# When the main heads' decay is laid out: after the seventh early step, not after the third

## The chip, the cores and the metric

The kernel runs on one core of one Trainium2 chip. The metric is device time in microseconds (us) of one launch. A core has five engines that work side by side and wait for each other through semaphores: TensorE (PE, matrix products), VectorE (DVE), ScalarE (ACT), GpSimd (POOL) and SyncE (SP), whose queue here issues every transfer (DMA).

## The reference

Attention with a forgetting gate on 8 batches of 8 heads, 576 positions and width 64, and behind it a feed-forward network on all 4608 tokens:

```python
scores = scale * np.matmul(q, k.transpose(0, 1, 3, 2))
log_f = np.log(np.clip(f, 0.0001, 1.0))
cum = np.cumsum(log_f, axis=-1)
decay = cum[:, :, :, None] - cum[:, :, None, :]
scores = np.where(causal, -1000000000.0, scores + decay)
...                                   # softmax over keys
attn_out = np.matmul(attn, v)
h = x @ w_in                          # x: 4608 x 512, w_in: 512 x 2048
g = np.maximum(0.01 * h, h)
return g @ w_out                      # w_out: 2048 x 512
```

The decay depends on `f` alone. Its running sum `cum` of a head is all that the scores need of it.

## The kernel before, in words

**Two phases.** The feed-forward network is most of TensorE's work, and it needs attention's results first. So the kernel begins with *early steps*: for the first 256 positions of three batches (`NE` = 3), one step for each pair of heads, twelve steps in all (`g` counts the four pairs of a batch). What these give is enough for the first feed-forward groups. Then come the *main heads*: 64 tasks, one a head, for the remaining positions, with feed-forward work filled in between.

**An early step.** `early_scores(b, g)` makes four score tiles (`sce_b_g_c`): a product of `qk` (L109, in float32) and one that adds the decay (L109, from the tile `both`). DVE takes each out of PSUM with its minimum (L303, into `ze`), which frees one of only two banks for the next score tile; ACT exponentiates (L307), DVE makes the reciprocal of the sums (L312, L313) and ACT scales the four tiles (L315). `early_values(b, g)` runs one step later: PE transposes the tiles (`tre`, L113), ACT copies them out of PSUM (`pte`, L327), PE multiplies by the values (`ave`, four matmuls that each copy `pte` feeds two of), ACT and DVE split the result into a high and a low part (`xh` L340, `xl` L341), from which the feed-forward network reads.

**Weights.** Between steps, `load_weight` unpacks one piece of the feed-forward weights (16 pieces of 1 MB, two transfers each, L163): two passes on ACT (L177 into `wt`, L185 into `win_h` or `wout_h`) and five on DVE (L180, L186, L187, L190, L191).

**Feed-forward quanta.** `fill(n)` sends up to `n` pieces of the feed-forward network: `h` matmuls (24 for a tile), then `g` (ACT L631), its split `gh` (DVE L634) and `gl` (DVE L636), then `o` matmuls. `FQ` is zero for the first four steps and then 4, 8, 8, ... `warm(n)` sends matmuls on zeros whose result nobody reads; they stand between the scores of the first six steps.

**The decay's second layout.** The early steps use the two tiles in `both`, made at the start. The main heads read the decay from DRAM instead, and `decay_rows` puts it there: it scales the running sums `fc` in place (DVE L226), takes each block's first value off (five DVE instructions, L231, into `start`), splits both into a high and a low part (ACT L209 and DVE L210 for `fck`, the same for `fcq`) and writes four halves to DRAM (SP L238, `dec_k` and `dec_q`). The first transfers that read them back belong to `split(0)` (L382, L383), called in the eleventh step; the first matmul on the tile that they fill starts at 151.5 us.

**What sets the order.** The code above gives a program order, and a scheduler in the language's framework reorders each engine's instructions by its own estimate of when operands and buffers are ready. A few instructions are pinned to program order; L226 is one. Each engine then runs its list strictly in that order, so an instruction that waits holds all that stand behind it.

```python
if x == 2:
    decay_rows()
if x:
    early_values(*steps[x - 1])
```

Of the kernel before, what the change touches and what calls it, by code (L numbers as in the profile page):

```python
# [38 lines left out]
def forgetting_attention_ffn(ctx, tc, qT, kT, v4, vr, f, w_in, w_out, out):  # L39
# [155 lines left out]
    def weights(n):  # L195
        while len(loaded) < min(n, len(wpieces)):
            load_weight(len(loaded))
# [25 lines left out]
    def decay_rows():  # L223

        tc.keep_in_program_order(
            nc.vector.tensor_scalar(fc, fc, -1.0 / SCALE, None, op0=ALU.mult)  # L226
        )
        start = one.tile([P, S], F32, tag="x", name="start")
        for i in range(NCH):
            c = slice(i * P, width(i))  # L230
            nc.vector.tensor_scalar(  # L231
                start[:, c], fc[:, c], 0.0, fc[:, i * P:i * P + 1], op0=ALU.mult, op1=ALU.subtract
            )
        for name, tag, x, to in (("fck", "s1", fc, dec_k), ("fcq", "m1", start, dec_q)):
            r = one.tile([P, S], F32R, tag=tag, name=name, bufs=2)
            halves(r, x)
            for w in range(2):
                nc.sync.dma_start(to[:, w], r[w * NHEAD:(w + 1) * NHEAD].bitcast(F32))  # L238
# [4 lines left out]
    def load(t):  # L243

        s, c0, c1 = tasks[t]
        h = state[t] = {}
        a, n = c0 * P, S
        x = h["raw"] = one.tile([P, S], F32, tag="qraw", name=f"raw_{t}")
        for y, src in ((x[:D, a:n], qT[s][:, a:n]), (x[D:, :n], kT[s][:, :n])):
            last = nc.sync.dma_start(y, src)  # L250
            if t < 2:
                tc.keep_in_program_order(last)
        if s % 2 == 0:
            pairs[s // 2, c0] = {}

    def load_v(t):

        g, o = tasks[t][0] // 2, tasks[t][0] % 2
        vm = fixed["vm"]
        for y, src in ((vm[:, :NFULL], v4[g][:, o]), (vm[:REST, NFULL], vr[g][:, o])):  # L260
            last = nc.sync.dma_start(y, src)
            if t < 1:
                tc.keep_in_program_order(last)
# [3 lines left out]
    def early_load(b, g):  # L267

        e = early[b, g] = {}
        x = e["qk"] = one.tile([P, 2, T], F32, tag="b2", name=f"qk_{b}_{g}", bufs=B2)  # L270
        for y, src in enumerate((qT, kT)):
            nc.sync.dma_start(
                x[:, y], src[b * HPB + 2 * g:b * HPB + 2 * g + 2, :, :T].rearrange("s d n -> (s d) n")
            )
        v = e["v"] = one.tile([P, 2, T // P, D], F32, tag="b2", name=f"ve_{b}_{g}", bufs=B2)
        nc.sync.dma_start(v, v4[b * HPB // 2 + g][:, :, :T // P])

    def early_scores(b, g):
        e = early[b, g]
        mx = one.tile([P, 4], F32, tag="max", name=f"maxe_{b}_{g}", bufs=3)  # L280
        sm = one.tile([P, 4], F32, tag="sum", name=f"sume_{b}_{g}", bufs=3)
        for i in range(2):
            n = width(i)
            ps = [
                psum.tile([P, 512], F32, tag="sc", name=f"sce_{b}_{g}_{2 * o + i}")[:, :n]
                for o in range(2)
            ]
            for o in range(2):
                x = e["qk"][o * D:(o + 1) * D]
                matmul(ps[o], x[:, 0, i * P:n], x[:, 1, :n], start=True, stop=False)  # L290
            for o in range(2):
                s = b * HPB + 2 * g + o
                matmul(
                    ps[o], pick[:, s:s + 1].broadcast_to([P, P]), decay_r[i],
                    start=False, stop=True,
                )
            for o in range(2):
                c = 2 * o + i
                tag = ZE[g % 2][c]
                z = e[c] = one.tile(  # L300
                    [P, n], F32, tag=tag, name=f"ze_{b}_{g}_{c}", bufs=BUFS.get(tag, 1)
                )
                nc.vector.tensor_tensor_reduce(  # L303
                    out=z, in0=ps[o], in1=tri[:, TRI - n:], scale=-SCALE, scalar=3.0e38,
                    op0=ALU.add, op1=ALU.min, accum_out=mx[:, c:c + 1],
                )
                nc.scalar.activation(  # L307
                    z, z, AF.Exp, bias=mx[:, c:c + 1], scale=-1.0, accum_out=sm[:, c:c + 1]
                )
            if b * HPB // 2 + g < WARM[2]:  # L310
                warm(WARM[1])
        nc.vector.tensor_scalar(sm, sm, 1.0e-9, None, op0=ALU.add)  # L312
        nc.vector.reciprocal(sm, sm)  # L313
        for c in range(4):
            nc.scalar.activation(e[c], e[c], AF.Copy, scale=sm[:, c:c + 1])  # L315

    def early_values(b, g):
        e = early[b, g]
        pts = []
        for o in range(2):  # L320
            ps = psum.tile([P, 512], F32, tag="tr", name=f"tre_{b}_{g}_{o}")
            for x, (c, j) in enumerate(((2 * o, 0), (2 * o + 1, 0), (2 * o + 1, 1))):
                transpose(
                    ps[:, x * P:(x + 1) * P], e[c][:, j * P:(j + 1) * P], ident
                )
            pt = one.tile([P, 3 * P], F32, tag=("z4", "e4")[o], name=f"pte_{b}_{g}_{o}")
            nc.scalar.copy(pt, ps[:, :3 * P])  # L327
            pts.append(pt)
        out = psum.tile([P, 512], F32, tag="tr", name=f"ave_{b}_{g}")
        for o, pt in enumerate(pts):  # L330
            rows_ = slice(o * D, (o + 1) * D)
            matmul(out[rows_, :T], e["v"][:, o, 0], pt[:, :T], start=True, stop=False)
            matmul(out[rows_, P:T], e["v"][:, o, 1], pt[:, T:], start=False, stop=True)
        if b not in groups:
            x = one.tile([P, T], F32, tag="x", name=f"xe_{b}_{g}")
            nc.scalar.copy(x, out[:, :T])
            nc.sync.dma_start(xd[g * P:(g + 1) * P, b * T:(b + 1) * T], x)
            return
        xh, xl = groups[b]
        nc.scalar.copy(xh[:, g, :], out[:, :T])  # L340
        nc.vector.tensor_tensor(xl[:, g, :], out[:, :T], xh[:, g, :].bitcast(F32), op=ALU.subtract)  # L341
# [22 lines left out]
    def split(t):  # L364


        s, c0, c1 = tasks[t]
        h = state[t]
        a, n = c0 * P, S
        x = "ab"[t % 2]  # L370
        s1 = h["s1"] = one.tile([P, S], F32R, tag="s1", name=f"s1_{t}", bufs=2)
        m1 = h["m1"] = one.tile([P, S], F32R, tag="m1", name=f"m1_{t}", bufs=2)
        s2, m2 = h["s2"], h["m2"] = fixed["s2" + x], fixed["m2" + x]
        raw = h["raw"]
        for y, x in ((s1[:D, a:n], raw[:D, a:n]), (m1[D:, :n], raw[D:, :n])):
            last = nc.scalar.copy(y, x)  # L376
            if t < 2:
                tc.keep_in_program_order(last)
        for y in (s1, s2):
            nc.sync.dma_start(y[D:, a:n].bitcast(F32), s1[:D, a:n].bitcast(F32))  # L380
        nc.sync.dma_start(m1[:D, :n].bitcast(F32), m1[D:, :n].bitcast(F32))
        nc.sync.dma_start(s2[2:4, a:n].bitcast(F32), dec_q[s][:, a:n])  # L382
        nc.sync.dma_start(m2[:2, :n].bitcast(F32), dec_k[s][:, :n])  # L383
        minus(m2[D:, :n], raw[D:, :n], m1[D:, :n].bitcast(F32))
        minus(s1[:D, a:n], raw[:D, a:n], s1[:D, a:n].bitcast(F32))
# [291 lines left out]
    def fill(n):  # L677

        settle()
        credit[0] += n  # L680
        while credit[0] >= 1:
            credit[0] -= 1
            if not next(quanta, None):
                credit[0] = 0
                return
            used[0] += 1
# [22 lines left out]
    for x, (b, g) in enumerate(steps + [(NE, 0)]):  # L709
        if x + 1 < len(steps):  # L710
            early_load(*steps[x + 1])
        if x < len(steps):
            early_scores(b, g)
            if x in (8, 11):
                load(x // 11)
            if x == 8:
                load_v(0)
            if x == 10:
                split(0)
            weights(sum(WQ[:x + 1]))  # L720
        if x == 2:
            decay_rows()
        if x:
            early_values(*steps[x - 1])
            if steps[x - 1][1] == HPB // 2 - 1:
                ready[0] = (steps[x - 1][0] + 1) * T
        if x == len(steps):
            split(1)
        fill(FQ[x])
# [73 lines left out]
```

## Time and profile before

| | |
|---|---|
| time, median of 3 runs | 1214.53 us (1214.12 to 1217.29) |
| the profiled execution's own time | 1215.27 us |
| its span, first to last instruction | 1213.2 us |
| mean granted TensorE clock over the span | 0.995 |
| PE busy | 1197.9 us (99%) |
| DVE, ACT, POOL busy | 619.5, 637.1, 460.5 us |
| transfers | 110.54 MB, mean 91 GB/s |

The profiled execution took 0.74 us more than the median. Its span is 2.07 us shorter than its time, which is what lies before the first and behind the last instruction.

A row of the timeline gives the start, the duration, the engine, the line, the operation, the tiles written and read, how many instructions are merged, and in brackets how long the engine stood idle before and whose end it waited for. A row of the windows gives a stretch, its length, the busy time of PE with the number of instructions that began there, the granted share of the TensorE clock, the transfers' share and their rate. Matmuls are pipelined and their ends are modelled, so short waits of PE hide in its busy time; an idle time that shows is a lower bound. A float32 matmul of the code stands as two in the trace.

### The profile page before, as it was taken

The numbers are of one execution on the slowest core, as the hardware profiler recorded it, in microseconds if no ns is written. First come the engines' busy times: TensorE is split into PE (matmuls) and PEld (weight loads), VectorE is DVE, ScalarE is ACT, GpSimd is POOL, SyncE is SP. The second block draws the span as 40 slices with busy tenths as digits, with TensorE's granted clock in tenths as the row PEclk, the third lists the DMA queues.
The fourth block names the chain that finished last, engine by engine and source line by source line (L and its number), as shares of the span: only waits on it lengthen the run. The fifth ranks groups of instructions, "written<-read, shape, count | busy, mean of one in ns | idle before, by whom it ended". The sixth has DMA issues, their size and how long they took to land.

```text
span 1213.2 us, 22495 instructions
## 1 busy us (share of the span) xinstructions
PE 1197.9 (99%) x7812; PEld 1070.6 (88%) x7812; DVE 619.5 (51%) x1685; ACT 637.1 (53%) x1633; POOL 460.5 (38%) x473
## 2 busy tenths in 40 slices
PE   9999999999999999999999999999999999999998
PEld 6677888888899999999999999999999999998997
DVE  5787756566655455554544444445444444553221
ACT  5776655667665565555545545455445445651111
POOL 1000155464555445454445353434454543531000
PEclk9899999999999999999999999999999999999999
DMA  5445433344343333323332323232223223221000
GB/s 183 140 172 182 125 109 103 90 124 120 97 126 91 84 97 92 110 80 89 92 99 64 90 71 95 70 90 63 74 84 88 62 69 82 76 62 46 19 18 18
DMA packets 82128, 110.54 MB, mean 91 GB/s; under 512 B 20640, under 2 KB 51728, under 8 KB 82016
## 3 DMA queue, kind: packets, MB, share of 16 engines
q1 hardware_dynamic: 82016, 109.12, 31.1%
q8 instruction: 62, 1.02, 0.4%
q14 instruction: 50, 0.41, 0.1%
HBM read 65.32 MB, written 18.58 MB: 69 GB/s over the span
## 4 chain that ended last, share of the span: by engine, by line
PE 94%; DVE 2%; DMA 1%; ACT 1%; issue 1%; POOL 0%; SPq 0%; DVEq 0%; ACTq 0%; POOLq 0%
PE h L109 33%; PE o L109 33%; PE tr L113 8%; PE av L109 8%; PE sc L109 7%; PE sce L109 2%; PE warm L109 2%; PE ave L109 1%; PE tre L113 1%; DVE fixed_z L414 0%; DMA wraw<-in_w_out 0%; DMA wraw<-in_w_in 0%; ACT g L631 0%; DVE gh L634 0%; DVE pl L466 0%
## 5 line engine op out<-in xcount | busy, mean ns | idle before, releaser
L636 POOL TENSOR_TENSOR gl<-g,gh 128x512 fp32r<-128x512 f32 x113 | 148.9, 1318 | 275.1 <-DVE gh L634 269.7
L109 PE MATMUL o<-wout_h,gh 128*128 128x512 f32 x576 | 231.3, 402 | 0.0
L109 PE MATMUL o<-wout_h,gl 128*128 128x512 f32 x576 | 227.3, 395 | 1.4 <-DVE gl L636 1.4
L109 PE MATMUL o<-wout_l,gh 128*128 128x512 f32 x576 | 227.5, 395 | 0.0
L420 ACT ACTIVATE fixed_z<-fixed_z,max 128x192 f32<-128x192 f32 (+3 forms) x272 | 161.0, 592 | 100.3 <-DVE max L414 98.0
L109 PE MATMUL h<-xh,win_h 128*128 128x256 f32 x1152 | 206.7, 286 | 0.9 <-ACT win_h L185 0.9
L464 ACT CAST ph<-tr 128x192 fp32r<-128x192 f32 (+3 forms) x360 | 126.8, 373 | 150.1 <-PE tr L113 99.5
L109 PE MATMUL h<-xh,win_l 128*128 128x256 f32 x1152 | 200.6, 283 | 0.1
L414 DVE CUSTOM_DVE_ANT_0 fixed_z<-sc,tri 128x192 f32<-128x192 f32 (+3 forms) x272 | 122.5, 452 | 151.0 <-PE sc L109 148.1
L631 ACT ACTIVATE g<-h 128x512 f32<-128x512 f32 x144 | 85.8, 596 | 216.3 <-PE h L109 200.1
L634 DVE CAST gh<-g 128x512 fp32r<-128x512 f32 x144 | 74.0, 514 | 214.4 <-ACT g L631 211.4
L466 DVE TENSOR_TENSOR pl<-tr,ph 128x384 fp32r<-128x384 f32 (+3 forms) x296 | 137.5, 467 | 81.6 <-ACT ph L464 80.2
L109 PEld LDWEIGHTS h<-xh,win_h 128*128 128x128 f32 x1152 | 171.2, 190 | 7.0 <-ACT win_h L185 1.0
L109 PEld LDWEIGHTS h<-xh,win_l 128*128 128x128 f32 x1152 | 165.2, 191 | 0.6 <-DVE win_l L191 0.3
L109 PE MATMUL h<-xs,win_h 128*128 128x256 f32 x1024 | 164.5, 283 | 0.0
L113 PE MATMUL tr<-ident_r,fixed_z 128*128 128x128 f32 x888 | 145.3, 274 | 3.5 <-DVE ph L471 1.7
L109 PEld LDWEIGHTS h<-xs,win_h 128*128 128x128 f32 x1024 | 141.0, 192 | 0.0
L109 PEld LDWEIGHTS o<-wout_h,gl 128*128 128x128 f32 x576 | 108.3, 188 | 26.2 <-DVE gl L636 2.1
L113 PEld LDWEIGHTS tr<-ident_r,fixed_z 128*128 128x128 f32 x888 | 107.7, 140 | 24.8 <-ACT rb L543 5.4
L109 PEld LDWEIGHTS o<-wout_l,gh 128*128 128x128 f32 x576 | 108.8, 189 | 15.8 <-issue 0.3
L150 POOL TENSOR_TENSOR fixed_m2a<-raw,m 64x576 fp32r<-64x576 f32 x32 | 46.0, 1437 | 202.1 <-ACT m L376 178.9
L109 PEld LDWEIGHTS o<-wout_h,gh 128*128 128x128 f32 x576 | 109.0, 189 | 15.0 <-issue 0.2
(110 smaller groups left out, 1761.5 us busy)
## 6 DMA issues: line engine op xcount, KB each, us to landing
raw<-in_kT SPq DMA_DIRECT2D x64, 144.0 KB
m<-m SPq DMA_DIRECT2D x64, 144.0 KB
wraw<-in_w_in SPq DMA_DIRECT2D x16, 512.0 KB
wraw<-in_w_out SPq DMA_DIRECT2D x16, 512.0 KB
fixed_vm<-in_v SPq DMA_DIRECT2D x64, 128.0 KB
xs<-xd SPq DMA_DIRECT2D x16, 512.0 KB
out<-ost SPq DMA_DIRECT2D x28, 256.0 KB
raw<-in_qT SPq DMA_DIRECT2D x40, 144.0 KB
```

What stands on the lines that cost most here:

```text
L109: nc.tensor.matmul(*args, **kw)
L113: nc.tensor.transpose(*args)
L150: nc.gpsimd.tensor_tensor(out, a, b, op=ALU.subtract)
L414: nc.vector.tensor_tensor_reduce(out=z[:, a:b], in0=ps[:m, :b - a], in1=tri[:m, at:at + b - a], scale=-SCALE, scalar=3.0e38 if x == 0 else ...
L420: nc.scalar.activation(z, z, AF.Exp, bias=h["max"][:m, last:last + 1], scale=-1.0, accum_out=fixed["sum" + "ab"[s // 2 % 2]][:m, i, s % 2: ...
L464: nc.scalar.copy(strided(ph, run), source(ps, run))
L466: nc.vector.tensor_tensor(strided(pl, run), source(ps, run), strided(ph, run).bitcast(F32), op=ALU.subtract)
L631: nc.scalar.activation(g, ph, AF.Prelu, alpha=0.01)
L634: nc.vector.tensor_copy(gh, g)
L636: eng.tensor_tensor(gl, g, gh.bitcast(F32), op=ALU.subtract)
```

## The change

`decay_rows()` is called in the seventh early step (`x == 6`) in place of the third (`x == 2`). No instruction is added or removed.

```diff
-        if x == 2:
+        if x == 6:
             decay_rows()
         if x:
             early_values(*steps[x - 1])
```

The scheduler then orders the engines differently from the fourth step to about the eleventh. In the rows that follow, a name ends in a number that only counts tiles; ahead of it stand, for the tiles of a step, the pair `g` and, for score tiles, which of the four it is (`ze_3_0` is the first tile of the fourth pair). The batch is left out: `g` 3 is the fourth step of the program here, and the `0` and `1` that follow it belong to the second batch, so the fifth and sixth step.

**First place: ACT at the old position.** Before, behind the fourth step's last exponential:

```order
L307 ACTIVATE ze_3_3_447,sume_3_420<-ze_3_3_447,maxe_3_419 128x256
L209 CAST fck<-fc 128x576
L177 ACTIVATE wt_464<-wraw_461 128x1024
L209 CAST fcq<-start 128x576
L327 COPY pte_2_0_476<-tre_2_0_472 128x384
L327 COPY pte_2_1_482<-tre_2_1_478 128x384
L185 CAST wout_h_115<-wt_464 128x1024
L315 ACTIVATE ze_3_0_427<-ze_3_0_427,sume_3_420 128x128
```

Now:

```order
L307 ACTIVATE ze_3_3_430,sume_3_403<-ze_3_3_430,maxe_3_402 128x256
L177 ACTIVATE wt_447<-wraw_444 128x1024
L315 ACTIVATE ze_3_0_410<-ze_3_0_410,sume_3_403 128x128
L315 ACTIVATE ze_3_1_427<-ze_3_1_427,sume_3_403 128x256
L315 ACTIVATE ze_3_2_413<-ze_3_2_413,sume_3_403 128x128
L315 ACTIVATE ze_3_3_430<-ze_3_3_430,sume_3_403 128x256
L185 CAST wout_h_115<-wt_447 128x1024
L327 COPY pte_2_0_459<-tre_2_0_455 128x384
L327 COPY pte_2_1_465<-tre_2_1_461 128x384
```

The two casts of the decay (`fck`, `fcq`) are gone from here. The copies `pte_2` stand behind the four scalings and the cast `wout_h` now; before, they stood ahead of both.

**Second place: PE and ACT one step on.** The matmuls between the two value products, before:

```order
L109 MATMUL ave_2_484<-pte_2_1_482,ve_2_249 64x128
L109 MATMUL sce_0_1_515<-qk_0_414 128x256
L109 MATMUL sce_0_1_515<-both 128x256
L113 MATMUL tre_3_0_549<-ident_r,ze_3_0_427 128x128
L113 MATMUL tre_3_0_549<-ident_r,ze_3_1_444 128x128 x2
L109 MATMUL sce_0_3_516<-qk_0_414 128x256
L109 MATMUL sce_0_3_516<-both 128x256
L109 MATMUL h_0_568<-xh_153,win_h_98 128x256
L109 MATMUL h_0_568<-xh_153,win_l_106 128x256
L109 MATMUL h_1_599<-xh_153,win_h_99 128x256
L109 MATMUL h_1_599<-xh_153,win_l_107 128x256
L113 MATMUL tre_3_1_555<-ident_r,ze_3_2_430 128x128
```

Now the last two score tiles of the fifth step (`sce_0_1`, `sce_0_3`) and the first of the sixth stand ahead of `ave_2`, the other three of the sixth ahead of the second half of `ave_3`, and `ave_3` is followed by a long run of `h` matmuls. Its surroundings now:

```order
L109 MATMUL sce_1_3_638<-qk_1_474 128x256
L109 MATMUL ave_3_544<-pte_3_0_536,ve_3_323 64x256
L109 MATMUL ave_3_544<-pte_3_0_536,ve_3_323 64x128
L109 MATMUL sce_1_3_638<-both 128x256
L109 MATMUL ave_3_544<-pte_3_1_542,ve_3_323 64x256
L109 MATMUL ave_3_544<-pte_3_1_542,ve_3_323 64x128
L113 MATMUL tre_0_0_671<-ident_r,ze_0_0_487 128x128
L113 MATMUL tre_0_0_671<-ident_r,ze_0_1_504 128x128 x2
L109 MATMUL h_0_551<-xh_153,win_h_98 128x256
L109 MATMUL h_0_551<-xh_153,win_l_106 128x256
```

On ACT, the two copies `pte_3` that `ave_3` reads stood side by side before:

```order
L340 CAST xh_153<-ave_2_484 128x256
L307 ACTIVATE ze_0_0_504,sume_0_497<-ze_0_0_504,maxe_0_496 128x128
L307 ACTIVATE ze_0_2_507,sume_0_497<-ze_0_2_507,maxe_0_496 128x128
L327 COPY pte_3_0_553<-tre_3_0_549 128x384
L327 COPY pte_3_1_559<-tre_3_1_555 128x384
L340 CAST xh_153<-ave_3_561 128x256
```

Now four scalings and a cast stand between them:

```order
L177 ACTIVATE wt_524<-wraw_521 128x1024
L327 COPY pte_3_0_536<-tre_3_0_532 128x384
L315 ACTIVATE ze_0_0_487<-ze_0_0_487,sume_0_480 128x128
L315 ACTIVATE ze_0_1_504<-ze_0_1_504,sume_0_480 128x256
L315 ACTIVATE ze_0_2_490<-ze_0_2_490,sume_0_480 128x128
L315 ACTIVATE ze_0_3_507<-ze_0_3_507,sume_0_480 128x256
L185 CAST win_h_100<-wt_524 128x1024
L327 COPY pte_3_1_542<-tre_3_1_538 128x384
L307 ACTIVATE ze_1_0_626,sume_1_619<-ze_1_0_626,maxe_1_618 128x128
L340 CAST xh_153<-ave_3_544 128x256
```

**Third place: DVE at the new position.** The decay now stands behind the unpacking of the weight piece `win_l_109`, among the seventh step's work:

```order
L190 TENSOR_SCALAR wraw_784<-wt_787 128x1024
L191 SCALAR_TENSOR_TENSOR win_l_109<-wraw_784 128x1024
L226 TENSOR_SCALAR fc<-fc 128x576
L231 TENSOR_SCALAR start<-fc 128x128 x4
L231 TENSOR_SCALAR start<-fc 128x64
L210 TENSOR_TENSOR fck<-fc,fck 64x576
L180 TENSOR_SCALAR wt_871<-wt_871 128x1024
L634 CAST gh_2_731<-g_2_729 128x512
L303 ISA ze_2_0_760,maxe_2_752<-sce_2_0_754,tri 128x128
L303 ISA maxe_2_752 128x1
L303 ISA ze_2_2_763,maxe_2_752<-sce_2_2_755,tri 128x128
L303 ISA maxe_2_752 128x1
```

Ahead of the decay stands what the next `h` matmuls read (`win_l_109`); behind it the split `gh_2` and the first score tiles of the seventh step (`ze_2_0`, `ze_2_2`), and `fcq` comes after these. On ACT, `fck` and `fcq` stand just ahead of `g_2`. On SP, the four writes to DRAM, which stood ahead of the second half of the fifth weight piece, stand between the two halves of the ninth.

## The prediction

> **What bounds the kernel now.** The page first: who is busy.
>
> ```profile
> PE 1197.9 (99%) x7812; PEld 1070.6 (88%) x7812; DVE 619.5 (51%) x1685; ACT 637.1 (53%) x1633; POOL 460.5 (38%) x473
> ```
>
> TensorE sets the end. Its work stays the same to the last matmul, so the time can change only by what PE waits and by the clock it runs at, and only in the first 110 us or so, where the orders differ. Next, PE in windows of 3.41 us around the old position of the decay, and one later window.
>
> ```profile
> 37.87:41.28 3.41, 1.72 (x11) 1.00 0.86 257
> 41.28:44.70 3.42, 3.37 (x12) 0.50 0.61 154
> 44.70:48.11 3.41, 3.41 (x13) 0.50 0.71 222
> 48.11:51.52 3.41, 3.41 (x14) 0.50 0.70 273
> 51.52:54.94 3.42, 3.42 (x24) 1.00 0.03 7
> 102.72:106.14 3.42, 2.21 (x10) 1.00 0.18 72
> ```
>
> This is the finding of the profile: after a window in which PE was busy for 1.72 of 3.41 us (0.50), the granted clock is 0.50 for 10.24 us. The window at 102.72 with 2.21 (0.65) had no such effect. So the point from which the clock falls lies, in this trace, between 0.50 and 0.65. Why the window was so empty is read from the chain of waits (its pieces in order of time) and from the timelines of PE and ACT.
>
> ```profile
> 38.02 0.37 DVE fc L226
> 38.72 0.95 DVE start L231 x5
> 39.70 0.76 DVE fck L210
> 41.28 0.77 DVE fcq L210
> ```
>
> ```profile
> 38.42 0.67 ACT L209 CAST fck<-fc 128x576 fp32r<-128x576 f32 x1
> 39.00 1.13 ACT L177 ACTIVATE wt<-wraw 128x1024 f32<-128x1024 f32 x1
> 40.04 0.65 ACT L209 CAST fcq<-start 128x576 fp32r<-128x576 f32 x1
> 40.60 0.84 ACT L327 COPY pte<-tre 128x384 f32<-128x384 f32 x2
> 41.34 1.05 ACT L185 CAST wout_h<-wt 128x1024 fp32r<-128x1024 f32 x1
> 42.34 1.50 ACT L315 ACTIVATE ze<-ze,sume 128x128 f32<-128x128 f32 x4
> ...
> 43.74 0.35 ACT L340 CAST xh<-ave 128x256 fp32r<-128x256 f32 x1
> 43.99 0.40 ACT L307 ACTIVATE ze<-ze,maxe 128x128 f32<-128x128 f32 x1
> ...
> 51.08 0.51 ACT L307 ACTIVATE ze<-ze,maxe 128x256 f32<-128x256 f32 x1
> ```
>
> ```profile
> 35.73 1.24 PE L109 MATMUL ave<-pte,ve 128*64 128x256 f32 x8
> 36.90 0.55 PE L113 MATMUL tre<-ident_r,ze 128*128 128x128 f32 x3
> ...
> 41.11 1.92 PE L109 MATMUL ave<-pte,ve 128*64 128x256 f32 x8 [1.55 <-ACT pte L327]
> 43.09 1.22 PE L109 MATMUL sce<-qk 64*128 64x256 f32 x2
> 44.23 0.58 PE L109 MATMUL sce<-both 128*128 128x256 f32 x1
> 44.61 0.84 PE L113 MATMUL tre<-ident_r,ze 128*128 128x128 f32 x3
> ...
> 48.54 2.24 PE L109 MATMUL ave<-pte,ve 128*64 128x256 f32 x8
> ```
>
> ACT casts `fck` and `fcq` before it copies `pte_2`, PE stands 1.55 us for that copy, and DVE meanwhile does 2.85 us of decay (0.37 + 0.95 + 0.76 + 0.77) ahead of the score tiles that PE needs next.
>
> **The change part by part.** *Removed, the slow clock (T1).* The same operations at full clock stand in the rows above (`ave` 1.24, `tre` 0.55) and in these:
>
> ```profile
> 30.73 0.70 PE L109 MATMUL sce<-qk 64*128 64x256 f32 x2
> 31.65 0.36 PE L109 MATMUL sce<-both 128*128 128x256 f32 x1
> ```
>
> In the slow stretch stand two `ave` (0.68 and 1.00 longer), two `sce<-qk` (0.52 each), two `sce<-both` (0.22 each) and two `tre` (0.29 each): 1.68 + 1.04 + 0.44 + 0.58 = 3.74. The bounds are 0, if ACT and DVE had held PE to the same pace, and half of 10.24, 5.12. I take 3.7: PE is busy for 10.19 of the 10.24 us, so its pace rules there. It goes away if the first window fills up. The gap of 1.55 us ran from 39.56. In the new order two more score tiles stand in it ahead of `ave_2`, at the price of this pair from the eighth step:
>
> ```profile
> 80.96 0.80 PE L109 MATMUL sce<-qk 64*128 64x256 f32 x4
> 81.69 0.50 PE L109 MATMUL sce<-both 128*128 128x256 f32 x2
> ```
>
> That is 1.3 us of work; the window comes to (1.72 + 1.3) / 3.41, some 0.85 without the start of `ave_2`, and the clock stays up.
>
> *Moved, the copies `pte_2` (T2).* They lose the two casts ahead (1.32) and get four scalings and `wout_h`: 38.42 + 1.13 + 1.50 + 1.05 = 42.1, and 0.3 for sums that DVE has ready later, so about 42.4 in place of 40.60. PE fills this 1.8 us with the 1.3 above and the first tile of the sixth step (about 0.4). Its idle time stays about what it was, in two pieces. I take -0.3; the bounds are +1.8, if nothing fills it, and -2.85, the decay's share of the chain, if all that DVE did there was on the path.
>
> *Added, a wait between the two `pte_3` (T3).* They stood together; now four scalings (1.50) and `win_h` (1.05) stand between. From the end of the first copy to the end of the second ACT takes 1.50 + 1.05 + 0.42 = 3.0 us (0.42: half of 0.84). PE has half an `ave` (0.62) and a `sce<-both` (0.36) for it, so it stands about 2.0 us. Then `h` waits for `xh` (0.35), of which `tre_0_0` hides most: 0.2 more. T3 = +2.2. Behind the second copy on ACT stand the exponentials of the sixth step, for which DVE and then the scalings wait; they are two tiles further than before, so that this costs PE nothing at once. Bounds: 0, if PE comes 2 us late to it, and 3.0.
>
> *Where T3 falls (T5).* On ACT from 42.4: copies 0.84, exponentials 2 x 0.40 and 2 x 0.51, `xh` 0.35, `wt` 1.13 and some 0.5 for `ave_2` give 47.0 for the first copy and 50.5 for the end of the second. PE's idle stretch, about 48.4 to 50.5, lies inside the window from 48.11 to 51.52: 1.2 of 3.41 us busy, under 0.50. So I expect the clock to fall again, at 51.52. There PE has 30 `h` matmuls and eight `warm` in a row. How soon dense work brings the clock back shows at the program's start, with the same kind of matmul slow and fast:
>
> ```profile
> 1.45 7.48 PE L109 MATMUL warm<-still 128*128 128x512 f32 x20 [1.45 <-DVE tables L102]
> 9.28 4.38 PE L109 MATMUL warm<-still 128*128 128x512 f32 x18
> ```
>
> At 4.38 / 18 = 0.243 each, twenty take 4.87; they took 2.61 longer, so 5.2 us ran slow: part of a window and one whole one. One window costs 3.41 / 2 = 1.7, since dense work doubles. T5 = +1.7; the bounds are 0 and 5.12 (three windows, as before).
>
> *Moved, the decay itself (T4).* DVE 2.85, ACT 1.32, and four writes on SP. At the new place, in five-us windows and two waits:
>
> ```profile
> 70.00:75.00 5.00, 4.99 (x31) 3.29 (x31) 3.66 (x9) 2.88 (x8) 0.00 (x0) 1.00 0.66 229
> 75.00:80.00 5.00, 4.91 (x37) 4.13 (x37) 4.71 (x12) 4.21 (x11) 0.00 (x0) 1.00 0.62 214
> 71.35 0.60 ACT L631 ACTIVATE g<-h 128x512 f32<-128x512 f32 x1 [1.54 <-PE o L109]
> 74.60 0.69 DVE L636 TENSOR_TENSOR gl<-g,gh 128x512 fp32r<-128x512 f32 x1 [1.27 <-PE sce L109]
> ```
>
> ACT has 2.12 us free in the first window, more than 1.32. DVE has 1.34 and 0.29, so 1.2 us of the 2.85 push what stands behind: `gh_2`, for which `o` waits, and `ze_2_0`, whose bank the next score tile waits for. PE's cover are the 24 `h` matmuls on `win_h_101`, whose inputs DVE has done ahead of the decay. I take +0.3; without that cover 1.2, and at most 2.85. SP's writes:
>
> ```profile
> 39.12 1.84 SPq L238 DMA_DIRECT2D dec_k<-fck x2
> 41.05 1.45 SPq L238 DMA_DIRECT2D dec_q<-fcq x2
> L109 PE MATMUL sc<-fixed_m2a,fixed_s2a x168: 272/295/454, 151.5 to 1078.4; 128*128 128x288 f32 x64, 128*128 128x320 f32 x32, 128*128 128x448 f32 x32, 128*128 128x64 f32 x20
> ```
>
> They hold the queue for 3.3 us. Before, values and half a weight piece queued behind them; now half of the ninth piece and the eighth step's loads do. The first reader of the decay starts at 151.5, some 70 us later. Cost 0; if the ninth piece came late, up to 3.3. POOL's order is unchanged.
>
> Sum: -3.7 - 0.3 + 2.2 + 1.7 + 0.3 = +0.2. The profiled execution took 1215.27, so 1215.5 by its own time; it lay 0.74 above the median, against which I forecast 1214.7: **no change that can be told.**
>
> [...]
>
> **The rivals.** *First: no second fall (faster).* Without T5 the sum is -1.5: 1213.0. With T2 at its far end it is -4.05, 1210.5. For it: the windows' grid need not lie the same in each execution, and an idle stretch of 2 us split over two windows leaves both above 0.65. Against it: with the grid of this trace the stretch falls into one. [...]
>
> *Second: the second fall lasts (slower).* If `h` waits for `xh` and for weight pieces within the slow stretch, the clock stays down for three windows as in the trace: T5 is 5.1, the sum +3.6, 1218.1, and with the decay's 1.2 uncovered 1219.0. It decides from the point where a window after 51.52 holds no more matmuls than the 12 or 13 in the two slow windows that did not end it. Against it: the 30 `h` have their weights.
>
> *Third: the change does not do what it says.* If the first window stays below the point (0.50 to 0.65), the clock falls at 41.28 as before, T1 is 0, the later wait lies in slow work, and the sum is -0.3 + 2.2 + 0.3 = +2.2: 1216.7.
>
> **How the numbers follow.** Forecast 0.42, first rival 0.33, second 0.12, third 0.09, none of these 0.04. About 0.3%, 3.6 us, is what can be told from no change: faster is below 1210.9, slower above 1218.2. Faster: four tenths of the first rival (T2 well towards its end, or T1 near 5.1) and most of the rest, 0.16. Slower: half of the second, a fifth of the third, the forecast's upper edge, 0.13. Same 0.71. The range goes from the first rival's far end, a little lower for T1's bound, to the second's: 1209.8 to 1218.2. The forecast's own is 1213 to 1216.5.
>
> **What would show it.** Clock 1.00 from 41.28 to 51.52 shows T1; a stretch of 0.50 some 3.4 us long from about 51.5 shows T5. A wait of `ave` for `pte` of about 2 us near 50 shows T3, with L315 and L185 ahead of it on ACT. The rows L226 to L210 near 70 to 80 with no new wait of PE beside them show T4. The forecast is wrong if the clock never falls, stays down for more than one window, or falls at 41.28 as before.

## The result and the profile after

The changed kernel takes 1207.95 us (median of 4 runs, 1207.86 to 1210.32), the kernel before 1214.98 (4 runs): a ratio of 0.9944 with an interval of 0.9925 to 0.9962. The forecast was 1214.7, no change, with a range from 1209.8 to 1218.2, so it was wrong: the kernel is faster by 0.56%, and its time lies below the range. A later comparison with more executions of both (the fifth experiment below) gave 1208.62 against 1213.80, a ratio of 0.9952 (0.9938 to 0.9966).

The profiled execution of the changed kernel is the longest of its four (1210.32, span 1208.2, mean clock 0.997). The other three have spans of 1205.8 to 1205.9 and clocks of 0.999 to 1.000.

The page's first part: TensorE is still the bound and 5.8 us less busy, with the same 7812 instructions.

```profile
PE 1192.1 (99%) x7812; PEld 1068.8 (88%) x7812; DVE 615.7 (51%) x1685; ACT 636.3 (53%) x1633; POOL 460.7 (38%) x473
```

PE in windows of 3.41 us of the changed kernel, on its own grid, steps of 3.413 us from the point where the clock rises (here 4.74, before 7.15: up to it a weight load of `warm` takes 330 ns in the median, behind it 188, in both profiles):

```profile
32.04:35.46 3.42, 2.52 (x15) 1.00 0.59 188
35.46:38.87 3.41, 3.41 (x18) 0.50 0.45 126
38.87:42.29 3.42, 2.54 (x15) 1.00 0.87 301
42.29:45.70 3.41, 3.41 (x22) 1.00 0.00 1
45.70:49.11 3.41, 2.32 (x12) 1.00 0.90 303
49.11:52.53 3.42, 3.33 (x23) 1.00 0.03 10
110.55:113.96 3.41, 2.12 (x15) 1.00 0.83 279
113.96:117.38 3.42, 3.42 (x17) 0.50 0.07 28
```

The slow stretch of 10.24 us behind the old decay is gone (T1 as expected), and there is none from 51.5 us either (T5 did not come). But the clock falls for one window at 35.46, in a place that both programs share, and once more at 113.96. Both falls stand behind windows that were 0.74 and 0.62 busy, fuller than the 0.50 that I had made the cause; the first is fuller even than the window of 0.65 behind which the clock did not fall before.

The timeline of PE where the waits were expected, and of ACT ahead of the second one:

```profile
34.25 0.39 PE L109 MATMUL h<-xh,win_h 128*128 128x256 f32 x1 [0.90 <-ACT win_h L185]
40.47 0.48 PE L109 MATMUL sce<-qk 64*128 64x128 f32 x2 [0.25 <-DVE maxe L303]
41.84 1.24 PE L109 MATMUL ave<-pte,ve 128*64 128x256 f32 x8 [0.63 <-ACT pte L327]
49.20 0.86 PE L109 MATMUL ave<-pte,ve 128*64 128x256 f32 x4 [1.18 <-ACT pte L327]
```

```profile
38.98 1.49 ACT L315 ACTIVATE ze<-ze,sume 128x128 f32<-128x128 f32 x4 [0.39 <-DVE sume L313]
40.38 1.03 ACT L185 CAST wout_h<-wt 128x1024 fp32r<-128x1024 f32 x1
41.32 0.84 ACT L327 COPY pte<-tre 128x384 f32<-128x384 f32 x2
...
45.43 0.46 ACT L327 COPY pte<-tre 128x384 f32<-128x384 f32 x1
46.34 1.50 ACT L315 ACTIVATE ze<-ze,sume 128x128 f32<-128x128 f32 x4 [0.45 <-DVE sume L313]
47.74 1.03 ACT L185 CAST win_h<-wt 128x1024 fp32r<-128x1024 f32 x1
48.68 0.47 ACT L327 COPY pte<-tre 128x384 f32<-128x384 f32 x1
```

The wait of 1.55 us for `pte_2` has become 0.63. The wait T3 is there, with the four scalings and `win_h` ahead of it as foreseen, but it is 1.18 us and not 2.0. And one row says more than both: the scalings of the fourth step start at 38.98, before at 42.34. With them the next step starts 3.4 us earlier (1.1 of it because this execution's clock rose 2.4 us earlier: its first twenty `warm` matmuls took 6.38 us, before 7.48), though PE's `ave_2` comes 0.7 us later. The scalings need the reciprocal of the sums from DVE, first before and then now:

```profile
42.07 0.18 DVE L313 RECIPROCAL sume<-sume 128x4 f32<-128x4 f32 x1
```

```profile
38.72 0.17 DVE L313 RECIPROCAL sume<-sume 128x4 f32<-128x4 f32 x1
```

Before, it stood behind `fcq`, the last piece of the decay on DVE, which started at 41.28; in both kernels the scalings start within 0.3 us of it. (Before, ACT too was busy up to that point, with the casts, the copies and `wout_h`.)

The decay at its new place, on DVE, and the windows of all engines there (busy time of PE, PEld, DVE, ACT and POOL with the number begun, then clock, transfers' share and rate):

```profile
64.29 0.45 DVE L226 TENSOR_SCALAR fc<-fc 128x576 f32<-128x576 f32 x1
64.77 1.04 DVE L231 TENSOR_SCALAR start<-fc 128x128 f32<-128x128 f32 x5
65.84 0.76 DVE L210 TENSOR_TENSOR fck<-fc,fck 64x576 fp32r<-64x576 f32 x1
...
68.11 0.76 DVE L210 TENSOR_TENSOR fcq<-start,fcq 64x576 fp32r<-64x576 f32 x1
```

```profile
60.00:65.00 5.00, 5.00 (x35) 4.61 (x34) 4.64 (x8) 1.85 (x3) 0.00 (x0) 1.00 0.74 265
65.00:70.00 5.00, 5.00 (x33) 3.66 (x32) 4.87 (x15) 4.18 (x10) 0.00 (x0) 1.00 0.64 194
```

DVE is full there (4.87 of 5), and PE shows no wait (5.00 of 5): the cover of `h` matmuls holds. A wait of PE follows a little later, for a load that stood on SP's queue behind the four writes (65.47 to 69.33) and half a weight piece (69.39 to 69.97):

```profile
75.55 0.49 PE L109 MATMUL sce<-qk 64*128 64x128 f32 x4 [0.64 <-DMA qk<-in_kT]
```

### The profile page after: what moved, and what is told of

Its sections match the earlier page's. It is cut to its first block, busy times and chain, and to the rows that moved or that the text cites. A ratio compares the mean times of both kernels' runs of the same rounds, so it can differ in the third digit from the quotient of the medians.

```text
span 1208.2 us, 22484 instructions
## 1 busy us (share of the span) xinstructions
PE 1192.1 (99%) x7812; PEld 1068.8 (88%) x7812; DVE 615.7 (51%) x1685; ACT 636.3 (53%) x1633; POOL 460.7 (38%) x473
## 4 chain that ended last, share of the span: by engine, by line
PE 93%; ACT 2%; DVE 2%; DMA 1%; issue 1%; POOL 0%; SPq 0%; ACTq 0%; DVEq 0%; POOLq 0%
PE h L109 33%; PE o L109 32%; PE tr L113 8%; PE av L109 8%; PE sc L109 7%; PE sce L109 2%; PE warm L109 1%; PE ave L109 1%; DMA wraw<-in_w_out 1%; PE tre L113 1%; ACT ze L315 0%; DVE fixed_z L414 0%; ACT g L631 0%; DMA qk<-in_kT 0%; DVE pl L466 0%
## 5 line engine op out<-in xcount | busy, mean ns | idle before, releaser
L109 PE MATMUL sc<-m,s 128*128 128x288 f32 (+1 forms) x336 | 120.6, 364 | 0.2
```

Of the source, the lines that this page charges most:

```text
L109: nc.tensor.matmul(*args, **kw)
```

## The experiments

All times are medians, and each comparison is with the kernel before on the same chip. Since the clock turned out to differ between executions of one kernel, I also give how many had a mean clock of 0.999 or 1.000 (at most one slow window, since one is 0.0014 of the span; in nine of the fourteen profiles the last 0.4 to 1.6 us are slow too).

**The clock alone.** The first experiment keeps the decay where it was and fills the wait.

```diff
+    def gap(n, x):
+        ps = psum.tile([P, 512], F32, tag="o0", name="gap", bufs=1)
+        for _ in range(n):
+            matmul(ps, x, still, start=True, stop=True)
...
+        if (b, g) == (0, 2):
+            gap(GAP, groups[b][1][:, 1, :P])
```

`GAP` is 6, and the call stands in `early_values`, ahead of the value products.

> The kernel before, with six matmuls on zeros put on TensorE just ahead of its 1.55 us wait for the copies pte_2 (six times 0.243 us = 1.46 us, as warm's run at full clock). The order of every engine is otherwise that of before, and the decay stays at its old place. Theory A (the removed fall of the clock is the larger part of the gain): the window at 37.87 goes from 0.50 to (1.72 + 1.46) / 3.41 = 0.93 busy, the clock stays at 1.00 to 51.5 and beyond, and the time falls by 3.7 (T1 as predicted) to 5.1 us (half of the slow 10.24): 1209.9 to 1211.3. Theory B (what counted was the decay's 2.85 us on VectorE and 1.32 us on ScalarE ahead of the copies; the clock only fell along with it): the clock stays up, but TensorE then waits for the same instructions of VectorE and ScalarE, and the time stays within 1 us of before. If the six matmuls do not run inside the wait but ahead of it and push what follows, up to 1.5 us longer than these.

Measured: 1210.96 against 1213.15, ratio 0.9984 (0.9973 to 0.9995); 10 of 12 runs at 0.999 or above. Windows of PE, PE's rows and DVE's (the line numbers of this kernel are one higher in PE's rows and six higher in DVE's):

```profile
38.48:41.89 3.41, 2.98 (x19) 1.00 0.80 263
41.89:45.31 3.42, 3.42 (x18) 1.00 0.80 235
```

```profile
38.51 1.65 PE L110 MATMUL gap<-still,xl 128*128 128x512 f32 x6
40.00 0.40 PE L110 MATMUL h<-xl,win_h 128*128 128x256 f32 x2
40.33 1.04 PE L110 MATMUL ave<-pte,ve 128*64 128x256 f32 x8
41.80 0.70 PE L110 MATMUL sce<-qk 64*128 64x256 f32 x2 [0.43 <-DVE maxe L309]
```

```profile
39.98 0.76 DVE L216 TENSOR_TENSOR fcq<-start,fcq 64x576 fp32r<-64x576 f32 x1
40.77 0.18 DVE L319 RECIPROCAL sume<-sume 128x4 f32<-128x4 f32 x1
40.86 0.68 DVE L192 TENSOR_SCALAR wraw<-wraw 128x1024 int32<-128x1024 int32 x1
41.45 0.28 DVE L309 CUSTOM_DVE_ANT_0 ze<-sce,tri 128x128 f32<-128x128 f32 x1
```

The clock stays at 1.00 from 38.48 to 45.31, with the decay still there, and some 2 us of the median are gained: theory A in part. Theory B is in part right too: the next score tile then waits 0.43 us for DVE, which has just done `fcq` and a pass over a weight piece. The changed kernel is still faster by more than 2 us, so the clock is not all.

**The old place filled again, the new order kept.** `decay_rows` is called twice; the first call scales by 1.0.

```diff
-        if x == 6:
-            decay_rows()
+        if x in (2, 6):
+            decay_rows(1.0 if x == 2 else -1.0 / SCALE)
```

> The changed kernel, with decay_rows called also at its old place, where it scales by 1.0 (so that the values of the second call are right): 2.85 us more of VectorE, 1.32 us more of ScalarE and four more writes, at the old place. Up to the seventh step the order on TensorE is that of before, to the row. Theories A and B: the early loss of before is back (the same 1.55 us wait, the clock 0.50 for about 10 us behind it), so 1214 to 1216. Theory C (part of the gain, 1.5 to 2 us, comes from the order of the eighth to eleventh steps, 80 to 110 us): the later order is partly that of the changed kernel, so 1212.5 to 1214. If the old place costs nothing: 1208 to 1209.

Measured: 1216.43 against 1213.15, ratio 1.0022 (1.0010 to 1.0034); none of 12 runs at 0.999. The early loss is back (25.46 us in the stage table further below, 26.13 before). In its profile the clock falls at 43.14, not behind the wait of 1.57 us that ends at 40.41 but behind the next one, of 0.71 us for DVE; it falls at 118.23 too. The kernel is even 3.3 us longer than the kernel before; in the profile that is lost behind the first `o` matmul (90.86 us from there to the 121st, with the second fall in it, against 87.6 and 88.1 before). Theory C, a gain of the later order that survives, is not seen.

**Other places.** `x == 8`, the ninth step, and `x == 4`, the fifth.

> The decay laid out in the ninth early step in place of the seventh (x == 8). TensorE's order is that of the changed kernel up to the seventh step and another one behind it. Theories A and B: the gain is made before 60 us, so the lead at the first o matmul is the same 5.2 us (about 4.1 beyond the earlier start), and the time lies within 1 us of the changed kernel's: 1207 to 1209. Theory C: the further 1.5 to 2 us that the changed kernel gains between 80 and 110 us depend on that very order and are lost or change sign: 1209 to 1211.

> The decay laid out in the fifth early step (x == 4). TensorE's order is that of the changed kernel through the fourth step and the wait between the two copies pte_3; the decay then stands in the fifth to sixth step, where no feed-forward work covers it yet. Theory A: the fall of the clock at 41.28 is gone, which is most of the gain; a new wait of at most 2.85 us, and with it possibly a fall: 1208.5 to 1212, with a clock of 1.00 at 41 to 51 us in either case. Theory B: the decay's 2.85 us on VectorE merely move to another place of the same chain, so the time is that of before less 1 us at the most: 1214 to 1215.

Measured: the ninth step 1207.98, ratio 0.9958 (0.9946 to 0.9970), all 5 runs at 1.000; the fifth step 1209.52, ratio 0.9977 (0.9964 to 0.9990), 6 of 8 runs at 0.999 or above and one, 1213.22, at 0.993. So for the clock it is enough that the decay leaves the fourth step. Between the seventh and the ninth step the place makes no difference that can be told, and some 1.5 us are lost in the fifth, where theory B had expected nearly all to be lost. A later order that must be the changed kernel's (theory C) is not needed.

**How often the clock falls.** The changed kernel and the kernel before, once more.

> The changed kernel itself, beside the kernel before on the same chip, to see how often its clock falls. Theory of the grid (a stretch of idle time makes the clock fall only if it lies in certain places of a 3.41 us window that runs free of the program): about a quarter of the executions with a mean clock of 0.998 or lower and 1.5 to 3 us longer, the others at 0.999 to 1.000 and 1207.6 to 1208.3; median 1207.8 to 1208.5. Of the kernel before about two thirds with falls, those without at 1210 to 1211. If instead the first runs of the changed kernel were lucky: median 1209 to 1211, half of the runs or more with falls.

> The kernel before itself, for a second profile with the 3.41 us grid at another place. Theory of the grid: the clock falls at the next point of the grid where a wait of 0.9 us or more begins 1.2 to 2 us behind the last one (waits of TensorE near 34, 39.5 and 103 us), and not where it begins within 0.9 us behind it or less than 1.1 us ahead of the next. If no wait lies so: no fall, and a time of 1210.0 to 1211.0. Theory of the busy share (a window less than 0.50 to 0.65 busy): a fall only behind the wait of 1.55 us, in each execution, and 1214 to 1217.

Measured: the changed kernel 1208.62 against 1213.80, 9 of 11 runs at 0.999 or above; the kernel before 1214.44, with the clock down from 41.13 for 10.24 us, its grid nearly that of the first profile. Over all runs made here the kernel before has 18 of 86 executions at 0.999 or above, median 1210.71, and 1213.76 over all; the changed kernel has 12 of 15, median 1207.95, and 1208.58 over all. Of the 5.2 us between the medians over all, 3.0 are that the kernel before usually falls (1213.76 - 1210.71), and 2.8 the order without a fall (1210.71 - 1207.95); the changed kernel's own few falls take 0.6 back. The second profile of the changed kernel shows the very fall that T5 foresaw:

```profile
45.88:49.29 3.41, 2.23 (x12) 1.00 0.88 308
49.29:52.71 3.42, 3.42 (x14) 0.50 0.02 5
```

It fell behind T3's wait. In the profile of the ninth step the same wait of 1.18 us lies in a window just as full, and nothing happens:

```profile
48.36:51.77 3.41, 2.23 (x13) 1.00 0.37 150
51.77:55.18 3.41, 3.41 (x29) 1.00 0.41 119
```

**T3 by itself.** In the changed kernel the fifth step's four scalings (L315, now in a function `early_scale`) are called behind the fourth step's values.

```diff
+        e["sm"] = sm
+        if (b, g) != (1, 0):
+            early_scale(b, g)
...
             early_values(*steps[x - 1])
+            if x == 4:
+                early_scale(1, 0)
```

> The changed kernel with the four scalings of the fifth step called behind the values of the fourth, so that both copies pte_3 stand together on ScalarE again; the wait of 1.18 us between them should be gone. If that wait is a loss as the prediction's T3 has it: 1.2 to 1.5 us less than the changed kernel, 1206.4 to 1206.8 where the clock does not fall. If TensorE would only have waited later for the same vector and scalar work: within 0.5 us of the changed kernel. If it is this wait that makes the clock fall in some runs, fewer runs below 0.999 than the changed kernel.

Measured: 1209.62 against 1213.80, ratio 0.9973 (0.9954 to 0.9993); the 9 runs of 11 at 0.999 or above have a median of 1209.15, against 1208.58 for the changed kernel's 9 on this chip. PE's rows:

```profile
47.38 0.88 PE L109 MATMUL ave<-pte,ve 128*64 128x256 f32 x8
...
48.98 0.39 PE L109 MATMUL h<-xh,win_h 128*128 128x256 f32 x1 [0.30 <-ACT xh L346]
...
50.57 0.39 PE L109 MATMUL h<-xl,win_h 128*128 128x256 f32 x1 [0.62 <-DVE xl L347]
```

The wait of 1.18 us is gone; two smaller ones stand in its place. Up to the first `o` matmul 1.0 us is gained (table below), and at the end nothing; where it is lost again, the traces do not show. The falls of the clock do not become rarer either: 2 of 11 runs are below 0.999, as in the changed kernel, and they fall further (1215.70 and 1218.09, at 0.991 and 0.990).

**The wait near 34 us filled,** on the ninth step's kernel, with four float32 matmuls of 128x128 on zeros.

```diff
+            if x == 4:
+                gap(4, early[0, 2][0])
```

> The decay in the ninth early step, and four small float32 matmuls (128x128, nobody reads their result) between the third and the fifth step's score tiles, into TensorE's wait of 0.90 us near 34 us, which both kernels share. Theory of the grid: no fall near 35 us in any run, all runs at 0.999 or 1.000; 1207.6 to 1208.2. If the four matmuls push the fifth step's scores and with them VectorE: up to 0.8 us longer, 1208.5 to 1209.

Measured: 1208.32 against 1213.80, ratio 0.9949 (0.9931 to 0.9967), all 7 runs at 0.999 or above and the longest 1208.71. The matmuls cost nothing that can be told, and with this wait filled no run of this kernel fell so far that its mean clock shows it.

**The order alone.** The first experiment with four matmuls (`GAP = 4`), and the changed kernel with the wait near 34 us filled.

> The kernel before with four matmuls on zeros (4 x 0.243 = 0.97 us) in place of six in its wait of 1.55 us, so that they end before the copies pte_2 do and delay nothing. The order of every engine is otherwise that of before, and the decay is at its old place. Theory D (of the median gain of some 5 us, about 3 are the fall of the clock that the kernel before has in most executions, and about 2 are the decay's 2.85 us of VectorE that leave the chain of the fourth and fifth step): no fall behind 39.5 us in any run, median 1209.8 to 1210.8, a little under the six matmuls' 1210.96, and still some 2 us longer than the changed kernel. If the clock is all of the gain: 1208 to 1208.6. If 0.97 us is too little to keep the clock up: 1212 to 1214 with clocks of 0.995 to 0.997.

> The changed kernel (decay in the seventh step) with the four small float32 matmuls in the wait of 0.90 us near 34 us. Theory of the grid: falls near 35 us are gone; those behind the wait of 1.18 us near 48 us (one of three profiles of the changed kernel's order so far) stay, so at most a fifth of the runs below 0.998; median 1207.8 to 1208.6, that is the changed kernel's, since most of its runs have no fall anyway. Beside the kernel of the four dummies above, both without falls, it gives the worth of the order alone: 2 us by theory D, 0 if the clock is everything.

Measured: 1210.82, ratio 0.9967 (0.9950 to 0.9983), and 1208.90, ratio 0.9956 (0.9942 to 0.9971), both against 1214.32. No run of the first was above 1212.04, as theory D has it. Both kernels still fall in other places: 4 of 12 runs of the first are below 0.999 and 1 of 12 of the second, and the profiles show falls at 35.16 and 100.02 in the first and at 114.30 in the second. The medians are 1.9 us apart, and those of the runs at 0.999 or above (1210.99 and 1208.85) 2.1: about that is what the order alone is worth here. The stage can be cut out of the traces, from the first matmul of `ave_1` (34 to 36 us) to the first `o`. The two ends of it in the kernel before, the first and the tenth experiment, in that order:

```profile
61.87 0.50 PE L109 MATMUL o<-wout_h,gh 128*128 128x512 f32 x1
```

```profile
34.44 0.84 PE L110 MATMUL ave<-pte,ve 128*64 128x256 f32 x4
...
57.22 0.50 PE L110 MATMUL o<-wout_h,gh 128*128 128x512 f32 x1
```

```profile
34.73 1.02 PE L109 MATMUL ave<-pte,ve 128*64 128x256 f32 x6
...
56.03 0.48 PE L109 MATMUL o<-wout_h,gh 128*128 128x512 f32 x1
```

| kernel | slow windows in the stage | ave_1 to first o |
|---|---|---|
| before, both profiles | three, from 41 | 26.13 |
| before with the wait filled (6, 4 and 4 matmuls) | one, near 35 | 22.77 |
| changed | one, at 35.5 | 21.91 |
| changed, second profile | two, at 35.6 and 49.3 | 23.15 |
| changed, wait near 34 filled; ninth step, with and without it filled | none | 21.29 |
| fifth step | none | 22.23 |
| both places, the second experiment | two, from 43.1 | 25.46 |
| changed without T3's wait; ninth step without both waits | none | 20.30 |

The slow window near 35 costs 21.91 - 21.29 = 0.62 in the new order. If it costs as much in the old one, the old order without any fall is 22.77 - 0.62 = 22.15, an estimate, and the order is worth 0.86 in this stage. The fifth step's 22.23 is no better than that: with the decay still ahead of the first `o`, the stage gains on balance from the clock alone.

**Both waits away, and the rest of the way.** The ninth step, the four matmuls near 34 us and the scalings called later, together; and the ninth experiment's kernel once more, for a trace.

> The decay in the ninth early step, the four small matmuls near 34 us, and the fifth step's scalings behind the fourth step's values, so that both copies pte_3 stand together: no wait of 0.90 and none of 1.18 us. If the 1.0 us that the removed wait gave up to the first o matmul can be kept when the decay comes two steps later: 1206.8 to 1207.6, faster than every kernel so far. If the vector and scalar work that the wait stood for is waited for later, as the median without the wait suggests: 1207.8 to 1209.

> The order of before with the four matmuls on zeros, once more, for a profile of the stretch from the first o matmul to the 121st. If the old order loses there by itself: 87.0 to 88.2 us without a fall of the clock in it (three profiles so far: 86.7, 87.6, 88.1), against 85.4 to 87.0 in the orders with the decay moved. If what TensorE waits for there, the transfers of weight pieces, varies by as much from run to run: anything from 85.5 to 88.2.

Measured: 1209.73 against 1213.17, ratio 0.9973 (0.9959 to 0.9987): not better than the changed kernel, and longer than either case expected. 4 of its 11 runs are below 0.999, though both waits are gone. The other, 1212.08, falls at 100.40, behind a wait of 1.70 us, so it does not decide between its two cases. The stretch from the first to the 121st `o` matmul takes, without a fall in it, 86.7 to 88.1 us in the old order (three profiles) and 85.4 to 87.0 in the six profiles with the decay moved; with one, 89.3 (twice, old) and 88.2 and 89.4 (new). So the rest of the order's gain, about 1 us, seems to lie here, but the two sets overlap and its cause is not settled. The longest wait of PE there has the same kind of cause in both, a weight piece that comes late: the transfer, then ACT's first pass, then DVE's, and behind DVE's the split `gl`. In the kernel before, on ACT, DVE and PE:

```profile
101.54 1.13 ACT L177 ACTIVATE wt<-wraw 128x1024 f32<-128x1024 f32 x1 [1.92 <-DMA wraw<-in_w_in]
```

```profile
102.71 0.69 DVE L180 TENSOR_SCALAR wt<-wt 128x1024 int32<-128x1024 int32 x1 [2.62 <-ACT wt L177]
103.31 0.69 DVE L186 TENSOR_SCALAR wraw<-wraw 128x1024 int32<-128x1024 int32 x1
103.92 0.69 DVE L636 TENSOR_TENSOR gl<-g,gh 128x512 fp32r<-128x512 f32 x1
```

```profile
104.66 0.50 PE L109 MATMUL o<-wout_h,gl 128*128 128x512 f32 x1 [1.21 <-DVE gl L636]
```

In the changed kernel the same kind of chain ends at a score tile:

```profile
110.89 1.13 ACT L177 ACTIVATE wt<-wraw 128x1024 f32<-128x1024 f32 x1 [3.71 <-DMA wraw<-in_w_out]
```

```profile
113.01 0.91 PE L109 MATMUL sce<-qk 64*128 64x256 f32 x4 [1.29 <-DVE maxe L303]
```

In the kernel before with its wait filled (6, 4 and 4 matmuls) the wait for `gl` was 0.74, 1.54 and 1.70 us, so it varies by a microsecond with hardly a change in the order.

## Why the prediction was wrong

**T1, the slow clock: right.** Forecast -3.7. The stage table gives 26.13 - 22.15 = 4.0, by the estimate above. The medians agree: executions of the kernel before with a mean clock of 0.995 or 0.996 (three windows are 0.0042 of the span) have 1214.30, those at 0.999 or above 1210.71, which is 3.6. What the forecast did not know is that a fifth of its executions have no such loss, and that another fifth (19 of 86, at 0.997 or 0.998) have a smaller one.

**T2, the copies and what the decay held up: the first step that failed.** Forecast -0.3, with -2.85 as the bound "if all that DVE did there was on the path". The order's 0.86 is T2 and T3 together; T3 costs 1.0 there (21.29 - 20.30), so T2 is about -1.9, a difference of differences that no run shows by itself. I had looked at PE's idle time, which indeed moved into two pieces, and not at when the next step's inputs come: the four scalings start 2.3 us earlier beyond the earlier start, and 2.9 in the ninth step's profile, which has no fall near 35 (39.57 against 42.34, with a start 0.12 later). Before, the reciprocal that they need stood behind the decay on DVE, and ACT was busy to the same point; in the new order both come free sooner. So the forecast's bound was the better guide: DVE's 2.85 us stood in the way of the next step, and a gain of some 1.9 reaches the first `o`. At the fifth step the same work costs 22.23 - 21.29 = 0.94 of the stage. How much of T2 comes from DVE's queue, and how much from ACT's two casts (1.32) and the new places of the copies, no run separates.

**T3, the wait between the copies: right in kind, wrong in size.** Forecast +2.2; the wait is 1.18 and costs 1.0 up to the first `o`. The second copy ended at 49.15 and not at 50.5, but 1.1 us of that is this execution's earlier start. Counted from the first matmul of `ave_1`, the wait was forecast from 12.7 to 14.8 us. It lies from 13.4 to 14.6 in the changed kernel's profile, which has the slow window near 35 ahead of it, and from 12.8 to 13.9 in the ninth step's, which has none. So without a fall PE came when forecast, and the second copy 0.8 us sooner: the first copy was forecast to start at 11.3 and started at 10.1, since ACT's work ahead of it was sooner done (T2 again). And the cost does not last to the end: without the wait the kernel is not faster.

**T5, the second fall: the second step that failed.** Forecast +1.7 with the chance of the likeliest case. It came in one of the six profiles that have this wait, and cost 23.15 - 21.91 = 1.24 there. The price of 1.7 had dense work take twice its time at a clock of 0.50, which no run shows: `h` matmuls begin 0.21 us apart in a slow window (second experiment, 45.56 to 46.20) and 0.12 in a fast one (changed kernel, from 107.81). My step was: a window 1.2 of 3.41 busy, under 0.50, therefore a fall. What failed is the 1.2: the window was 2.32 of 3.41 busy, and 0.65 to 0.68 in all six profiles, since the wait is shorter than forecast; between 0.56 and 0.74 the clock fell behind 8 windows of all profiles and not behind 20 (last section). Nor could this trace's grid place the wait. The grid lies differently in each execution, as the first rival's ground had it: the clock rose at 7.15 and 7.00 in the two profiles of before, and between 4.35 and 7.40 in the others.

**T4, the decay at its new place: right in kind.** Forecast +0.3. From the first to the 25th `o` matmul, over the decay, the changed kernel takes 16.60 us; the kernel before, without it there and with four small `ave` matmuls fewer, 16.56; the ninth step's, which has it later, 16.72. So DVE's and ACT's part costs nothing that can be told. SP's part was put at 0, and may not be: of the four profiles with the decay in the seventh step alone, two show PE waiting for `qk` just behind it (0.64 us, and 1.10 in the tenth experiment); in the other twelve such a wait is at most 0.21. That the writes cause it is not shown.

**The sum.** By the runs -4.0 - 1.9 + 1.0 + 0 + 0 = -4.9 up to the first `o` (T5 at 0, as in five of six profiles), against the forecast's +0.2, and about 1 more behind it, which the forecast did not consider since the orders differ little there. T5 (1.7), T2 (1.6) and T3 (1.2) make up most of the error. The first rival (no second fall, T2 at its far end: 1210.5) was the case that came, and was given 0.33; its price had T2 at -2.85 and T3 at +2.2, two errors that nearly cancel, and lacked that last microsecond. The third rival fell: with the pair of score tiles in it the window from 38.87 was 0.74 busy (2.54 of 3.42), and the clock stayed at 1.00 behind it.

A fall did not need a wait of 1.55 us: five profiles show one behind a single wait of 0.90 us: the changed kernel's two and those of the first, ninth and twelfth experiments. In the fourteen profiles the clock first rises between 4.35 and 7.40 us, and each later change inside the program lies a whole number of 3.413 us behind that: 10 and 13 of them in the first profile of before (41.28 and 51.52), 9, 10, 32 and 33 in the changed kernel's.

## What to carry to other kernels

Before a fall of the clock is priced, look at the mean clock of many executions: here the same program had a median of 1210.71 us in the fifth of them that hardly fell, and between 1213.1 (mean clock 0.997) and 1218.9 (0.993) in the others, and what a change does to the median is the price times the share. Work that leaves the chain of the next step on VectorE and ScalarE can be worth much of its duration (here some 1.9 us, with 2.85 gone from VectorE), even where the main engine's wait only seems to move; ask when the next step's inputs come, not how long this wait is. And a new wait need not be a loss at the end: here removing it gained 1.0 us at the first `o` and nothing over the whole.

## What the runs showed of the hardware that was not expected

Behind the same wait, in windows equally full, the clock fell in some executions and not in others. The wait of 0.90 us near 34 us is the same in eleven profiles. It began 1.22, 1.23, 1.31, 1.44 and 1.51 us behind a point of the grid in five, and the clock fell at the next point each time; it began 0.00, 0.07, 0.33, 0.85, 3.29 and 3.35 us behind one in six, and never did. The windows were equally full in all eleven (0.74 to 0.75). Behind the wait of 1.18 us near 48 us, in six profiles, it fell where the wait began at 2.17, and not at 0.25, 0.69, 1.04, 1.47 and 2.32 (there it ran over the point). So where the wait began and whether the clock fell went together near 34 us; but behind a wait that began at 1.4 to 1.5 the clock fell there (1.44 and 1.51) and not near 48 (1.47), and place alone does not account for it. When the window moves, other work comes to lie in it too, and no run holds that fixed.

How full the window was went with the falls only at the ends. Of all windows at full clock in the fourteen profiles (up to 1200 us), six were less than 0.56 busy, and the clock fell behind each; it fell behind none that was over 0.74; between these it fell behind 8 and not behind 20. PE's busy time is modelled, so the shares are rough, and what decides between these is not shown.

One slow window cost 0.62 us near 35 us (21.91 - 21.29; in the changed kernel's profile TensorE is busy for 2.54 of the 3.42 us behind it) and 1.24 near 49 (23.15 - 21.91).
